# Row sums of an attention softmax: five key blocks on the PE in 384 and 192 columns

## The chip, the cores and the metric

The kernel runs on one core of a Trainium2 chip. The metric is the device time of one execution in microseconds (us), as the median of several runs. The engines are PE (TensorE, matmul), DVE (VectorE), ACT (ScalarE), POOL (GpSimd) and SP (SyncE, which issues every DMA of this kernel, in program order).

## The reference

Three layers follow one another: a causal attention with a forget gate, a dense layer, and a layer of soft experts. Only the attention is touched by the change. It has 4 x 8 = 32 heads of 576 positions and 64 dimensions.

```python
scores = scale * np.matmul(q, k.transpose(0, 1, 3, 2))
log_f = np.log(np.clip(f, 0.0001, 1.0))
cum = np.cumsum(log_f, axis=-1)
decay = cum[:, :, :, None] - cum[:, :, None, :]
scores = np.where(causal, -1000000000.0, scores + decay)
scores = scores - np.max(scores, axis=-1, keepdims=True)
attn = np.exp(scores)
attn = attn / (np.sum(attn, axis=-1, keepdims=True) + 1e-09)
return np.matmul(attn, v)
...
x = attention output, 2304 x 512
h = x @ w_in; g = h * sigmoid(h); y = g @ w_out
soft experts on y: 32 slots, 8 experts, 2304 x 512 out
```

## The kernel before, in words

**Order.** Attention goes head by head: step `i` of `att_step` works on the scores of head `i`, on the row maxima of head `i + 3`, on the splitting of Q and K of head `i + 4`, and on the product with V of the pair of heads `pa` before. A pair takes two steps. The order of the pieces within a step is written out by hand in the string `ORDER` (L18), whose two halves, divided by a bar, are the first and the second step of a pair. Every engine carries out its instructions in that order. In the background the steps also convert a few of the dense layer's weights (`c`).

**Scores.** They are kept transposed: keys on the partitions, queries along the free axis. A head has five key blocks of 128, 128, 128, 128 and 64 keys; because of the causal mask block `kb` holds queries 128 kb to 576 only, so the blocks have 576, 448, 320, 192 and 64 columns. `s_piece` makes two matmuls a piece, ACT takes the exponential from PSUM into SBUF tiles `E[i][kb]` (L244), and POOL zeroes the upper triangle of the diagonal block (L246). `max_piece` (L190 on PE, L196 on DVE) does the row maxima of a later head in three PSUM banks taken in turn (ring "b"), from which `row_sums` takes its bank too.

**Row sums before.** The denominator of the softmax is the sum of `E` over keys, so over partitions and blocks. `e_sum` (L249 to L255, pieces `a0` and `a1` of the step after) adds blocks 0, 1 and 2 on DVE into a tile `ES`. `row_sums` (L262, piece `r` in the first step of a pair) then sums over the partitions with matmuls against a matrix of ones, 32 columns wide, so that four column groups of the PE hold two heads times two halves of 288 queries. Blocks 3 and 4 come from `E` directly. All operands are fp32, and the trace has two MATMUL instructions for each of these matmuls. ACT copies the 128 x 288 result to `RS` (L278), and one DMA spreads one row of each group over a tile `sg` of 128 partitions and 9 columns (L281). The step after, `norm_b` (L308 to L318, piece `n`) takes the reciprocal on DVE, stores it to a DRAM tile `R` with one DMA (L311) and reads it back twice, spread over 64 partitions each (`RB`, L318). `norm_c` (piece `b`) multiplies on DVE (L327).

**Queue behind the gather.** On SP the DMA of `sg` is followed by the load of Q and K of pair `p + 3` (`load`, piece `l0`, L139) into one of two buffers. `split_hi` (pieces `q0`, `q1`; L154 to L158 on ACT) reads that buffer from the beginning of the next pair's first step on.

Of the kernel before, what the change touches and what calls it, by code (L numbers as in the profile page):

```python
# [9 lines left out]
F32 = mybir.dt.float32  # L10
# [3 lines left out]
AF = mybir.ActivationFunctionType  # L14
ALU = mybir.AluOpType
AX = mybir.AxisListType

ORDER = "v0 m0 q0 v1 v2 a0 m1 m2 s0 s1 f0 a1 m3 a2 q1 z0 p s2 a3 s3 m4 r s4 l0 s5 c m5 z1 f1 | q1 q0 v0 v1 s0 l1 f0 f1 s1 a0 s2 z0 b a1 n v2 m0 m1 v3 m2 w s3 m3 s4 a2 z1 m4 s5 m5 a3 c"  # L18
NSUM = 1
# [19 lines left out]
def tile_attention_moe_softmoe(ctx: ExitStack, tc: tile.TileContext, qk, vr, f, wcat, phi, w1, w2, out):  # L39
# [23 lines left out]
    def bank(ring, shape, name):  # L63
        tags = RINGS[ring]
        turn[ring] += 1
        ch = tags[turn[ring] % len(tags)]
        return ps.tile(shape, F32, name=name, tag=("av" if ch in "ab" else "b") + ch, bufs=1)
# [59 lines left out]
    def load(p):  # L127
        b, hp = divmod(p, NP)
        src = qk[b, hp]
        if p == 0:  # L130
            staged[p] = ([UB[:, h] for h in range(2)],
                         [att.tile([128, S], F32, name="ES", tag="ES", bufs=2) for h in range(2)])
            nc.sync.dma_start(out=UB, in_=src[:, 0])
            for h in range(2):
                nc.sync.dma_start(out=staged[p][1][h], in_=src[:, 1, h])
            return
        t = ld.tile([128, 2, 2, S], F32, name="qk", tag="qk", bufs=2)
        staged[p] = [[t[:, c, h] for h in range(2)] for c in range(2)]
        nc.sync.dma_start(out=t, in_=src)  # L139
# [82 lines left out]
    E, ES = {}, {}  # L222
# [26 lines left out]
    def e_sum(i, j):  # L249
        if j == 0:  # L250
            ES[i] = att.tile([128, S], F32, name="ES", tag="ES", bufs=2)
        kb = j + 1
        m = 64 if kb == 4 else 128
        es = ES[i][0:m, 128 * kb:S]
        nc.vector.tensor_tensor(es, E[i][0][0:m, 128:S] if j == 0 else es, E[i][kb][0:m], ALU.add)  # L255

    AVP, U, RT = {}, {}, {}
    SUMS, READY, done = set(), set(), {"r": 0, "n": 0, "b": 0}
    HALF = S // 2
    ES_ = "sum"  # L260

    def row_sums(p):  # L262
        t = bank(RING_T, [128, HALF], "rs")
        parts = [(0, 128, HALF - 128, ES_), (0, 0, 128, 0), (1, HALF, HALF, ES_)]
        parts += [(1, 128 * kb, S - 128 * kb, kb) for kb in range(2 + NSUM, 5)]
        for half, c0, n, src in parts:
            for h in range(2):
                g = 32 * (2 * h + half)
                i = 2 * p + h
                k = 64 if src == 4 else 128  # L270
                rhs = ES[i][:, c0:c0 + n] if src is ES_ else E[i][src][0:k, 0:n]
                c = c0 - half * HALF
                nc.tensor.matmul(t[g:g + 32, c:c + n], lhsT=ones[0:k], rhs=rhs, start=src in (ES_, 0),  # L273
                                 stop=src == 0 or half == 0 or src == (4 if NSUM < 3 else ES_))
        for h in range(2):
            ES.pop(2 * p + h)
        r = att.tile([128, HALF], F32, name="RS", tag="RS", bufs=1)
        nc.scalar.activation(r, t, AF.Copy)  # L278
        sg = nrm.tile([128, 9], F32, name="sg", tag="sg", bufs=2)
        src = bass.AP(tensor=r.tensor, offset=r.offset, ap=[[32 * r.ap[0][0], 4], [1, HALF]])  # L280
        nc.sync.dma_start(out=sg, in_=src)  # L281
        RT[p] = sg
# [23 lines left out]
    def norm_b(p):  # L306
# [4 lines left out]
        nc.sync.dma_start(out=r.rearrange("h (c j) -> (h c) j", j=9), in_=sg)  # L311
# [17 lines left out]
    def att_step(i, cv):  # L329
# [22 lines left out]
        for op in ORDER.split("|")[h].split():  # L352
# [10 lines left out]
            elif k == "a" and 0 <= i - 1 < NH:  # L363
                if int(j) <= NSUM:
                    e_sum(i - 1, int(j))
                if j == "3":
                    SUMS.add(i - 1)
# [689 lines left out]
```

## Time and profile before

| | us |
|---|---|
| median of 3 runs | 629.3 (626.63 to 632.15) |
| profiled execution | 633.63 |
| its span, first to last instruction | 631.9 |
| PE busy | 562.0 (89%) |
| DVE busy | 421.9 (67%) |
| ACT busy | 348.7 (55%) |
| POOL busy | 262.4 (42%) |

The span leaves out what lies around the first and last instruction, so it is a little under the profiled execution's own time. Busy shares are means over the whole span; attention takes about its first 230 us, and the dense layer and the experts the rest. A busy PE is not a PE at its peak, since pipelined matmuls overlap and the end of each is modelled.

### The profile page before, as it was taken

How to read it: one execution, taken by the hardware profiler on the slowest of the kernel's cores; microseconds unless marked ns; L12 is line 12 of the kernel's file. 1: busy time of each engine (PE TensorE's matmuls, PEld its weight loads, DVE VectorE, ACT ScalarE, POOL GpSimd, SP SyncE). 2: the span in 40 equal slices, each digit the busy share in tenths (PEclk: the TensorE clock that was granted, in tenths of full speed). 3: DMA queues.
4: the chain of work that ended last, by engine and by line, in shares of the span. 5: the costliest groups of instructions: out<-in, count | busy, mean ns of one | idle time of the engine just before them, and what ended most of it. 6: DMA issues, size and time to landing. Idle time of an engine off the chain costs nothing.

```text
span 631.9 us, 13040 instructions
## 1 busy us (share of the span) xinstructions
PE 562.0 (89%) x4873; PEld 424.9 (67%) x4873; DVE 421.9 (67%) x1018; ACT 348.7 (55%) x783; POOL 262.4 (42%) x326
## 2 busy tenths in 40 slices
PE   3599999898998976989988999899999999978993
PEld 2476666565565655878876998777888989864542
DVE  7589999999987859999994114668768752322012
ACT  6688898887875656555654334354544633322022
POOL 6369879977967314564442000114334320002000
PEclk9999999999987998798998999999999999999997
DMA  6643564554542138511200022226423126697998
GB/s 207 212 161 129 179 222 133 177 164 155 175 133 65 43 120 297 188 67 67 80 23 0 3 67 67 68 67 233 167 68 129 44 95 198 207 332 263 349 350 273
DMA packets 46098, 94.44 MB, mean 149 GB/s; under 512 B 7858, under 2 KB 29138, under 8 KB 44114
## 3 DMA queue, kind: packets, MB, share of 16 engines
q1 hardware_dynamic: 46034, 93.61, 44.7%
q8 instruction: 38, 0.62, 0.4%
q14 instruction: 26, 0.21, 0.1%
HBM read 87.83 MB, written 4.94 MB: 147 GB/s over the span
## 4 chain that ended last, share of the span: by engine, by line
PE 54%; DVE 22%; ACT 9%; issue 7%; DMA 6%; SPq 0%; POOL 0%; ACTq 0%; DVEq 0%; POOLq 0%
PE h L557 8%; PE h L558 7%; PE h L559 7%; PE av L293 5%; PE mx L190 5%; PE gtp L590 4%; DVE wt L458 3%; DVE g L577 3%; PE st L239 3%; PE lp L604 3%; PE h L779 2%; PE st L241 2%; DVE ES L255 2%; PE rs L273 2%; DVE raw L462 2%
## 5 line engine op out<-in xcount | busy, mean ns | idle before, releaser
L557 PE MATMUL h<-xh,w 128*128 128x256 f32 x576 | 171.8, 298 | 2.0 <-ACT xh L544 2.0
L558 PE MATMUL h<-xl,w 128*128 128x256 f32 x576 | 164.3, 285 | 0.2 <-DVE xl L545 0.2
L559 PE MATMUL h<-xh,w 128*128 128x256 f32 x576 | 164.0, 285 | 0.0
L557 PEld LDWEIGHTS h<-xh,w 128*128 128x128 f32 x576 | 111.3, 193 | 19.4 <-issue 16.0
L577 DVE SCALAR_TENSOR_TENSOR g<-g,h 128x512 f32<-128x512 f32 (+1 forms) x73 | 49.3, 677 | 102.0 <-ACT g L571 102.0
L485 POOL TENSOR_TENSOR raw<-raw 128x512 f32<-128x512 f32 x32 | 40.9, 1279 | 175.5 <-DVE raw L464 99.9
L558 PEld LDWEIGHTS h<-xl,w 128*128 128x128 f32 x576 | 111.5, 194 | 0.4 <-DVE xl L545 0.4
L559 PEld LDWEIGHTS h<-xh,w 128*128 128x128 f32 x576 | 111.3, 193 | 0.0
L593 ACT ACTIVATE gt<-gtp 128x512 f32<-128x512 f32 x72 | 42.4, 589 | 85.9 <-PE gtp L590 85.7
L190 PE MATMUL mx<-KA,QA 127*128 127x256 f32 (+2 forms) x192 | 68.2, 399 | 23.7 <-DMA KA<-cum 9.3
L244 ACT ACTIVATE E<-st 128x256 f32<-128x256 f32 (+2 forms) x192 | 65.0, 382 | 29.1 <-PE st L241 26.9
L196 DVE CUSTOM_DVE_ANT_0 junk<-mx,mask 128x64 bf16<-128x64 f32 (+4 forms) x160 | 63.6, 421 | 21.6 <-PE mx L190 20.7
L246 POOL TENSOR_SCALAR_AFFINE_SELECT E<-E 128x128 f32<-128x128 f32 (+1 forms) x160 | 57.5, 376 | 47.6 <-ACT E L244 41.8
L190 PEld LDWEIGHTS mx<-KA,QA 127*128 127x128 f32 x192 | 38.0, 213 | 48.7 <-issue 17.9
L590 PE MATMUL gtp<-ident,g 128*128 128x128 f32 x288 | 45.5, 282 | 20.7 <-DVE g L577 16.2
L293 PE MATMUL av<-E,VF 128*64 128x320 f32 (+4 forms) x448 | 62.5, 386 | 0.0
L239 PE MATMUL st<-QA,KA 128*128 128x256 f32 (+1 forms) x192 | 61.3, 329 | 0.2
L241 PE MATMUL st<-QB,KB 128*128 128x256 f32 (+1 forms) x192 | 55.8, 305 | 0.0
L458 DVE SCALAR_TENSOR_TENSOR wt<-raw,wt 128x512 int32<-128x512 int32 x48 | 51.8, 1102 | 1.4 <-ACT wt L451 1.4
L451 ACT ACTIVATE wt<-wt,nbias 128x512 int32<-128x512 int32 x48 | 33.5, 720 | 34.6 <-DVE wt L448 34.4
L590 PEld LDWEIGHTS gtp<-ident,g 128*128 128x128 f32 x288 | 33.4, 143 | 23.9 <-DVE g L577 18.8
L168 POOL TENSOR_TENSOR QB<-qk,QB 64x576 fp32r<-64x576 f32 x30 | 43.0, 1434 | 8.2 <-ACT QB L158 5.9
(149 smaller groups left out, 994.5 us busy)
## 6 DMA issues: line engine op xcount, KB each, us to landing
unit<-in_w_dram SPq DMA_DIRECT2D x64, 512.0 KB
raw<-in_w_dram SPq DMA_DIRECT2D x48, 512.0 KB
qk<-in_qk_dram SPq DMA_DIRECT2D x15, 1152.0 KB
VF<-in_v_dram SPq DMA_DIRECT2D x16, 320.0 KB
RB<-R SPq DMA_DIRECT2D x32, 144.0 KB
out_dram<-ob SPq DMA_DIRECT2D x16, 256.0 KB
QA<-QA SPq DMA_DIRECT2D x2, 320.0 KB
UB<-in_qk_dram SPq DMA_DIRECT2D x1, 576.0 KB
```

Source lines behind the costliest of these rows:

```text
L190: nc.tensor.matmul(t[:, 0:n], lhsT=qa[0:127, h, 128 * blk:128 * blk + 128], rhs=ka[0:127, h, k0:k0 + n], start=True, stop=True)
L196: nc.vector.tensor_tensor_reduce(out=junk[:, 0:w], in0=t[:, 0:w], in1=mask[:, 448 - w:448], scale=1.0, scalar=-3e38, op0=ALU.add, op1=ALU.max,
L239: nc.tensor.matmul(t[0:m, 0:n], lhsT=ka[:, h, k0:k0 + m], rhs=qa[:, h, 64 + q0:64 + q1], start=True, stop=False)
L241: nc.tensor.matmul(t[0:m, 0:n], lhsT=kb_[:, h, k0:k0 + m], rhs=qb[:, h, q0:q1], start=False, stop=True)
L244: nc.scalar.activation(e[0:m, c0:c0 + n - skip], t[0:m, skip:n], AF.Exp, scale=0.125)
L293: nc.tensor.matmul(AVP[p][x][64 * h:64 * h + 64, o0:o0 + n], lhsT=VF[p % 2][0:k, kb, h], rhs=E[2 * p + h][kb][0:k, c:c + n], start=kb == 0 ...
L458: v.scalar_tensor_tensor(t, hi, -2147483648, t, op0=ALU.bitwise_and, op1=ALU.bitwise_or)
L557: nc.tensor.matmul(t[:, u], lhsT=a, rhs=xh[:, d], start=(d == 0), stop=False)
L558: nc.tensor.matmul(t[:, u], lhsT=a, rhs=xl[:, d], start=False, stop=False)
L559: nc.tensor.matmul(t[:, u], lhsT=w[:, 1, d * 128:(d + 1) * 128], rhs=xh[:, d], start=False, stop=(d == 3))
L577: nc.vector.scalar_tensor_tensor(g[:, u], g[:, u], 1.0, t[:, u], op0=ALU.add, op1=ALU.mult)
L590: nc.tensor.transpose(tp[:, t, u], g[:, u, t * 128:(t + 1) * 128], ident)
```

## The change

The adds on DVE go: `e_sum`, `ES`, and the pieces `a0`, `a1` (and `a2`, which did nothing) of `ORDER`. `a3` stays and only marks a head as complete. `row_sums` reads all five blocks of both heads from `E`. It cuts the 576 queries at 384: two column groups hold the first 384 queries of the two heads (blocks 0, 1, 2), two hold the last 192 (all five blocks). The copy on ACT, the gather into `sg` (now 96 partitions of 12 columns) and the store to `R` are two instructions each. The tile that holds K of the first pair keeps its size under another name.

```diff
-ORDER = "v0 m0 q0 v1 v2 a0 m1 m2 s0 s1 f0 a1 m3 a2 q1 z0 p s2 a3 s3 m4 r s4 l0 s5 c m5 z1 f1 | q1 q0 v0 v1 s0 l1 f0 f1 s1 a0 s2 z0 b a1 n v2 m0 m1 v3 m2 w s3 m3 s4 a2 z1 m4 s5 m5 a3 c"
-NSUM = 1
+ORDER = "v0 m0 q0 v1 v2 m1 m2 s0 s1 f0 m3 q1 z0 p s2 a3 s3 m4 r s4 l0 s5 c m5 z1 f1 | q1 q0 v0 v1 s0 l1 f0 f1 s1 s2 z0 b n v2 m0 m1 v3 m2 w s3 m3 s4 z1 m4 s5 m5 a3 c"
...
-    def e_sum(i, j):
-        if j == 0:
-            ES[i] = att.tile([128, S], F32, name="ES", tag="ES", bufs=2)
-        kb = j + 1
-        m = 64 if kb == 4 else 128
-        es = ES[i][0:m, 128 * kb:S]
-        nc.vector.tensor_tensor(es, E[i][0][0:m, 128:S] if j == 0 else es, E[i][kb][0:m], ALU.add)
...
-    HALF = S // 2
-    ES_ = "sum"
+    CUT = 384
 
     def row_sums(p):
-        t = bank(RING_T, [128, HALF], "rs")
-        parts = [(0, 128, HALF - 128, ES_), (0, 0, 128, 0), (1, HALF, HALF, ES_)]
-        parts += [(1, 128 * kb, S - 128 * kb, kb) for kb in range(2 + NSUM, 5)]
-        for half, c0, n, src in parts:
-            for h in range(2):
-                g = 32 * (2 * h + half)
...
-        nc.scalar.activation(r, t, AF.Copy)
-        sg = nrm.tile([128, 9], F32, name="sg", tag="sg", bufs=2)
-        src = bass.AP(tensor=r.tensor, offset=r.offset, ap=[[32 * r.ap[0][0], 4], [1, HALF]])
-        nc.sync.dma_start(out=sg, in_=src)
+        t = bank(RING_T, [128, CUT], "rs")
+        for kb in range(5):
+            k = 64 if kb == 4 else 128
+            for half, c0, c1 in ((0, 0, CUT), (1, CUT, S)):
+                q0 = max(c0, 128 * kb)
+                for h in range(2):
+                    g = 32 * (2 * half + h)
+                    if q0 < c1:
+                        nc.tensor.matmul(t[g:g + 32, q0 - c0:c1 - c0], lhsT=ones[0:k],
+                                         rhs=E[2 * p + h][kb][0:k, q0 - 128 * kb:c1 - 128 * kb], start=kb == 0,
+                                         stop=kb == (2, 4)[half])
+        r = att.tile([128, CUT], F32, name="RS", tag="RS", bufs=1)
+        nc.scalar.activation(r[0:64], t[0:64], AF.Copy)
+        nc.scalar.activation(r[64:128, 0:S - CUT], t[64:128, 0:S - CUT], AF.Copy)
+        sg = nrm.tile([96, 12], F32, name="sg", tag="sg", bufs=2)
+        for half, p0, n in ((0, 0, CUT), (1, 64, S - CUT)):
+            row = r[64 * half:64 * half + 1]
+            src = bass.AP(tensor=row.tensor, offset=row.offset, ap=[[32 * r.ap[0][0], 2], [1, n]])
+            nc.sync.dma_start(out=sg[p0:p0 + n // 6], in_=src)
...
-        nc.sync.dma_start(out=r.rearrange("h (c j) -> (h c) j", j=9), in_=sg)
+        for c0, c1, p0 in ((0, CUT, 0), (CUT, S, 64)):
+            nc.sync.dma_start(out=r[:, c0:c1].rearrange("h (c j) -> h c j", j=12), in_=sg[p0:p0 + (c1 - c0) // 6])
...
             elif k == "a" and 0 <= i - 1 < NH:
-                if int(j) <= NSUM:
-                    e_sum(i - 1, int(j))
-                if j == "3":
-                    SUMS.add(i - 1)
+                SUMS.add(i - 1)
```

## Rows read from the trace of the kernel before

**Rows 1.** The page: shares of the chain that ended last, by engine.

```profile
PE 54%; DVE 22%; ACT 9%; issue 7%; DMA 6%; SPq 0%; POOL 0%; ACTq 0%; DVEq 0%; POOLq 0%
```

**Rows 2.** Windows: length, busy PE, PEld, DVE, ACT, POOL; granted clock; DMA.

```profile
48.57:121.56 72.99, 69.33 (x512) 44.66 (x510) 70.54 (x207) 63.73 (x154) 64.41 (x91) 1.00 0.53 173
121.56:160.89 39.33, 35.96 (x259) 22.29 (x255) 37.38 (x108) 31.67 (x76) 30.73 (x45) 1.00 0.48 154
160.89:227.76 66.87, 61.05 (x429) 40.41 (x429) 53.99 (x152) 45.88 (x117) 41.52 (x69) 0.90 0.31 97
...
167.00:179.00 12.00, 10.96 (x56) 7.31 (x59) 10.36 (x30) 7.54 (x19) 8.44 (x13) 0.72 0.46 154
194.00:207.00 13.00, 10.76 (x56) 7.20 (x60) 9.95 (x29) 5.59 (x16) 7.17 (x12) 0.74 0.16 49
178.90:190.08 11.18, 11.18 (x87) 7.31 (x86) 10.47 (x32) 10.29 (x25) 8.96 (x14) 1.00 0.43 137
```

**Rows 3.** Timeline of ACT: start us, us; the first AV half's copy, one a pair.

```profile
48.57 0.36 ACT L298 ACTIVATE UB<-av 128x256 f32<-128x256 f32 x1
...
121.56 0.38 ACT L298 ACTIVATE UB<-av 128x256 f32<-128x256 f32 x1 [0.15 <-PE av L293]
```

**Rows 4.** The adds in the groups by line; then the chain in three stages.

```profile
L255 DVE TENSOR_TENSOR ES<-E 128x448 f32<-128x448 f32 x32 | 32.6, 1019 | 1.5 <-POOL E L246 1.5
L255 DVE TENSOR_TENSOR ES<-ES,E 128x320 f32<-128x320 f32 x32 | 21.4, 669 | 0.5 <-POOL E L246 0.2
...
by line: PE mx L190 13.7%; issue 12.3%; PE av L293 10.9%; DVE ES L255 8.8%; DVE junk L196 7.0%; DVE raw L462 6.0%; DVE x L327 5.6%; PE st L239 5.0%; PE st L241 4.9%; ACT E L244 4.2%; PE rs L273 3.7%; DVE wt L458 2.6%; DVE Mx L193 2.0%; ACT 
by line: DMA qk<-in_qk_dram 16.7%; issue 14.5%; DVE wt L458 9.1%; PE av L293 8.8%; PE rs L273 6.9%; DVE ES L255 6.6%; PE mx L190 6.3%; DVE junk L196 5.6%; PE st L239 5.3%; DVE x L327 4.9%; PE st L241 3.3%; ACT E L244 2.3%; DVE raw L460 2.2%
by line: PE av L293 23.2%; PE mx L190 14.6%; PE st L239 12.5%; PE st L241 9.5%; PE rs L273 9.1%; DVE x L327 5.8%; issue 4.8%; DVE ES L255 4.3%; DVE sg L308 2.3%; DVE junk L196 2.2%; PE h L558 1.8%; PE h L559 1.4%; DVE Mt L209 1.3%; PE h L55
```

**Rows 5.** Waits between 38 and 160.89: us in total, times, longest.

```profile
PEld rs L273 <- DVE ES L255: 3.8, 7, 1.2
ACT QA L157 <- DMA qk<-in_qk_dram: 3.1, 4, 1.4
ACT RS L278 <- issue: 3.0, 2, 1.6
```

**Rows 6.** Timeline of PE around one call of row_sums; chain in the expert layer.

```profile
178.91 0.70 PE L273 MATMUL rs<-ES,ones 128*32 128x160 f32 x7
...
180.10 0.39 PE L239 MATMUL st<-QA,KA 128*128 128x256 f32 x1
...
579.31 8.84 PE h L779 x160
```

**Rows 7.** Timeline of ACT over one pair: start us, us.

```profile
96.88 0.68 ACT L157 ACTIVATE QA<-qk 64x576 fp32r<-64x576 f32 x1 [1.39 <-DMA qk<-in_qk_dram]
...
101.15 0.41 ACT L278 ACTIVATE RS<-rs 128x288 f32<-128x288 f32 x1
...
108.44 0.67 ACT L157 ACTIVATE QA<-qk 64x576 fp32r<-64x576 f32 x1
```

**Rows 8.** Groups by line: copies of ACT from PSUM; busy us, mean ns.

```profile
L300 ACT ACTIVATE UB<-av 128x320 f32<-128x320 f32 x16 | 6.6, 415 | 3.3 <-PE av L293 3.3
...
L298 ACT ACTIVATE UB<-av 128x256 f32<-128x256 f32 x16 | 5.9, 370 | 6.2 <-PE av L293 6.2
```

**Rows 9.** Timeline of SP's queue in that pair: start us, us of issue.

```profile
101.59 0.62 SPq L281 DMA_DIRECT2D sg<-RS  x1
102.30 0.43 SPq L139 DMA_DIRECT2D qk<-in_qk_dram  x1
...
106.67 0.34 SPq L311 DMA_DIRECT2D R<-sg  x1
```

**Rows 10.** The chain before the second fall of the clock: start us, us.

```profile
195.01 1.81 DVE x L327 x2
196.82 0.75 DVE ES L255
```

More of the change, by code (lines that the diff above doesn't have):

```diff
@@ L131, in load @@
             staged[p] = ([UB[:, h] for h in range(2)],
-                         [att.tile([128, S], F32, name="ES", tag="ES", bufs=2) for h in range(2)])
+                         [att.tile([128, S], F32, name="k0", tag="k0", bufs=2) for h in range(2)])
             nc.sync.dma_start(out=UB, in_=src[:, 0])
@@ L220, in max_fin_b @@
                           in_=mr[0:5 * n].bitcast(F32))
-    E, ES = {}, {}
+    E = {}
     SP = [(0, 0, 256, 0), (0, 256, 576, 0), (1, 128, 576, 0), (2, 256, 576, 0), (3, 320, 576, 64), (4, 512, 576, 0)]
@@ L260, in tile_attention_moe_softmoe @@
-    ES_ = "sum"
+    CUT = 384
     def row_sums(p):
-        t = bank(RING_T, [128, HALF], "rs")
-        parts = [(0, 128, HALF - 128, ES_), (0, 0, 128, 0), (1, HALF, HALF, ES_)]
-        parts += [(1, 128 * kb, S - 128 * kb, kb) for kb in range(2 + NSUM, 5)]
-        for half, c0, n, src in parts:
-            for h in range(2):
-                g = 32 * (2 * h + half)
[L269 to L277, printed above, removed]
-        nc.scalar.activation(r, t, AF.Copy)
-        sg = nrm.tile([128, 9], F32, name="sg", tag="sg", bufs=2)
-        src = bass.AP(tensor=r.tensor, offset=r.offset, ap=[[32 * r.ap[0][0], 4], [1, HALF]])
-        nc.sync.dma_start(out=sg, in_=src)
+        t = bank(RING_T, [128, CUT], "rs")
[17 more added lines that the diff above has]
+            nc.sync.dma_start(out=sg[p0:p0 + n // 6], in_=src)
```

## The prediction

> **What bounds the kernel now.** I read the page's chain of waits first [rows 1]: PE has 54% of the path, DVE 22%, ACT 9%. The change touches attention only, so I then cut the span there by stage [rows 2], at the starts of the copy of the first AV half (L298), one per pair of heads; the first and the last of the seven of stage 1 stand in [rows 3], and the bounds of the later stages are the next such copies. Six pairs take 72.99 us, 12.17 each, with DVE busy 70.54 of it (11.76 a pair, 97%) and PE 69.33. Three more take 39.33 (13.11 each, DVE 95%); the last five, with less work per pair, 66.87. In stage 1 DVE has no slack; PE is close behind, but its busy time includes the tail of pipelined matmuls, so I looked for a pair in which PE never waits: from 178.90 to 190.08 it is busy for 11.18 of 11.18 us [rows 2]. That is PE's floor for a pair as it is now, 1.0 us under what stage 1 takes.
>
> The chain by stage [rows 4] says what the removed work holds: the adds (DVE ES L255) are 8.8% of stage 1 (6.4 us), 6.6% of stage 2 (2.6 us) and 4.3% of stage 3 (2.9 us): 11.9 us of the path, the most that can come back from them directly. Row sums on PE (rs L273) are 3.7%, 6.9% and 9.1%, or 2.7, 2.7 and 6.1 us.
>
> **Removed: the adds.** 32.6 + 21.4 = 54.0 us of DVE over 16 pairs [rows 4], 3.38 a pair. DVE falls from 11.76 to 8.4 us a pair in stage 1 and stops being the bound. The rs matmuls no longer wait for DVE: 3.8 us over 7 waits between 38 and 160.89 [rows 5]. The DVE steps behind the adds in program order (multiply x, reciprocal sg, the next max pieces) start up to 3.4 us earlier in a pair, and with them the PE pieces that wait for a bank of theirs.
>
> **Added on PE.** One call of row_sums starts at 178.91 and the next full-width matmul follows at 180.10: 1.19 us [rows 6]. Each fp32 matmul is two passes. The busier pair of its four column groups carries 288 + 192 + 64 columns, 1088 over two passes; the other pair 576. What a column costs with four groups side by side is read from the expert layer, 160 passes of 256 columns in 8.84 us [rows 6]: 55 ns each, so 221 ns for four at once and 0.863 ns a column in a group. 1088 columns make 0.94 us, and 0.25 us are start, the change to 64 rows and the drain. After the change the groups carry 384 + 256 + 128 = 768 and 4 x 192 + 64 = 832 columns; the busier one needs 1664 x 0.863 = 1.44, with the same 0.25 it is 1.69 us: **+0.50 us a pair**. Bounds: below, +0.50 less the wait for DVE that goes (3.8 over 7 is 0.54), so nothing; above, if the groups do not overlap more than one block with the next, 3200 x 0.863 + 0.25 = 3.01 us, +1.82. I take +0.50, since the old call itself fits the rate of the expert layer.
>
> **Added on ACT.** One copy of 288 columns, 0.41 us [rows 7], becomes one of 384 and one of 192. Copies of 320 and 256 columns take 415 and 370 ns [rows 8], 0.70 ns a column: 460 + 325 = 785, **+0.37 us a pair**. ACT is 63.73 of 72.99 busy in stage 1. At least nothing (other work of PE goes on), at most 14 x 0.37 = 5.2 us. In the three stages I count it on the path in three pairs: +1.2. Behind these copies on ACT stand the exponentials of the step's last pieces and the splits of Q and K.
>
> **Added on SP.** The gather of the sums (sg) is one issue of 0.62 us and becomes two; the store R 0.34, also two [rows 9]. Right behind sg on SP is the load of the Q and K of a later pair (L139). Its bytes come back at the head of the next pair, where ACT waits for them (L157): 3.1 us in 4 waits [rows 5]. The cost is between nothing (the first gather can be issued while ACT copies the second half) and 0.62 a pair; I take nothing for the forecast, because in that window of ten pairs it waited 4 times only, and keep the other end as a rival. The second R costs 0.34 in front of the last weight loads after attention: +0.4, at least nothing. The new shape of sg (96 x 12 for 128 x 9) changes two small DVE operations; the time that the removed adds leave on DVE covers that, and without it the next max pieces would wait for them as they do now.
>
> **The sum.** Stage 1: PE's floor becomes 11.18 + 0.50 = 11.68; 6 x (12.17 - 11.68) = -2.9. Stage 2: two copies of the sums came so late there that ACT stood 3.0 us [rows 5], behind adds that ended late. Floor plus 0.3 for a load that is still late, 12.0 a pair: -3.3. Stage 3: the adds on the path go (-2.9), five row sums get longer (+2.5), and the clock counts. The granted clock there is 0.72 over 167 to 179 and 0.74 over 194 to 207 [rows 2]: TensorE at the lower of its levels (1.2 for 2.4 GHz) for part of each, after PE had been idle (it is busy 10.96 of 12 and 10.76 of 13). (1 - 0.72) x 12 and (1 - 0.74) x 13 are 3.4 us each of full-speed time. Ahead of the second fall the path lies on DVE, with multiply and add one after the other [rows 10]; I count one of the two falls as saved, -3.4. Stage 3: -3.8. With +1.2 (ACT) and +0.4 (R): **-8.4 us**. Everything behind attention shifts with it. The profiled execution took 633.63 (span 631.9 and 1.73 around it), 4.3 above the median 629.3; its sum gives 625.2, and against the median 620.9. I predict **621 us**.
>
> **Rivals.** *PE is the bound already, and DVE's relief turns into DVE idle time.* For: PE busy 69.33 of 72.99, and the longer row sums lie where PE never waits. Against: the floor of 11.18 has room for 0.50. Stage 1 and 2 then give only half, -3.1, stage 3 -0.4 (adds against row sums, no clock), +1.6 elsewhere: about -2, **627 us**.
>
> *The chain of the next load becomes the bound (slower).* In one pair ACT's split starts at 96.88, the sums are copied at 101.15 [rows 7], the load is issued at 102.30 [rows 9], and the next split starts, without a wait, at 108.44: 11.56 us round. With +0.50 (PE), +0.37 (ACT) and up to +0.62 (second gather) it is 12.4 to 13.1, more than the 12.17 of a pair. At +0.9 for each of the 12 pairs with a load behind the gather it is +11: **640 us**. It decides once the bytes land after ACT reaches the split, which they did 4 times. Against: the rs wait that goes takes about 0.5 out of the same round, and the load may have landed well before 108.44. The Trainium skill ("DMA: Bandwidth & Descriptors", Rules for kernel authors) advises against two transfers to separate partition halves, because they serialize: by that the whole second issue counts, and the round would stand at the upper end. No row shows two gathers in a row.
>
> *DVE's relief comes in full and the clock stays up.* -11.9 for the adds, -6.8 for both falls of the clock, +4 for row sums and copies on the path: -15, **614 us**. For: the idle time of PE ahead of the second fall is DVE's [rows 10].
>
> *The four groups do not run side by side.* If each second pass held up all that is behind it, a call would take the 3.01 us above, and the floor 13.0 a pair: +5 in stage 1, nothing in stage 2, +9 in stage 3, +4 in the first pairs, **647 us**. The Trainium skill ("TensorE: Matmul & The Clock Gate", Step-by-step: what each phase is for) has it that matmuls stay in program order and only weight loads are pulled ahead. The 55 ns per pass of 256 columns [rows 6] speak against it: that order would give twice as much.
>
> **How the numbers follow.** Forecast 0.45, PE bound 0.28, load chain 0.13, full relief 0.10, no overlap 0.04. The range takes in the first, second and fourth case, with ACT's upper bound (+4 on 627) as its upper end: **613 to 632**; the slower two, 0.17, are left out. A measurement of this kernel can tell about 1% from no change, so 623.0 and 635.6 are the marks. The forecast, within some 4 us of its sum, lies below 623 with about 0.8 (0.36), the full relief always: faster 0.46. Same: the rest of the forecast and the PE rival, 0.37, and a little of the load chain, 0.39 in all. Slower: 0.15.
>
> **What would show it.** Right: DVE near 8.4 us a pair in stage 1 and PE nearly without idle time; rs calls of about 1.7 us that start without a wait; pairs of 11.7; no lower clock before 228 us or one fall fewer; the attention part 8 us shorter and the rest as before. Wrong: rs calls near 3 us; ACT's split waiting for the load in most pairs; pairs still at 12.1 with DVE idle; a clock that falls somewhere else, in attention or in the stage of converting weights behind it, and takes back what attention gained.

## The result and the profile after

| | before | after |
|---|---|---|
| median of 20 runs, us | 630.67 (626.63 to 636.82) | 624.61 (620.78 to 628.47) |
| ratio, 95% interval | | 0.9896 [0.9873, 0.992] |
| profiled execution, us | 633.63 | 622.81 |
| PE / DVE / ACT busy, us | 562.0 / 421.9 / 348.7 | 555.2 / 379.3 / 355.0 |

The kernel became 6.1 us faster by the medians, whose quotient is 0.9904; the ratio in the table is an estimate of its own. The prediction was 621 in a range of 613 to 632, from a sum of -8.4. The two profiled executions differ by 10.8, more than the medians, so the trace has to be read by stage before any of it is believed.

The page after: busy time and share of each engine, then the chain that ended last by engine.

```profile
PE 555.2 (89%) x5065; PEld 424.3 (68%) x5065; DVE 379.3 (61%) x954; ACT 355.0 (57%) x799; POOL 256.8 (41%) x326
...
PE 56%; DVE 16%; ACT 13%; DMA 6%; issue 5%; POOL 1%; SPq 1%; ACTq 0%; DVEq 0%; POOLq 0%
```

Against [rows 1] DVE lost 6 points of the path, PE took 2 of them and ACT 4. That ACT took twice what PE did is a first sign of where the forecast erred.

Windows of after, columns as in [rows 2]: the start, the three stages (cut at the same copy of the first AV half, now L288), the 112.24 us behind attention (weight conversion), the last 292 us (they overlap the stretch before by 3.3), and the two stretches of time in which the clock had fallen before the change.

```profile
0.00:50.82 50.82, 32.45 (x167) 22.66 (x167) 29.56 (x100) 35.50 (x71) 27.45 (x43) 1.00 0.55 180
50.82:125.71 74.89, 70.47 (x592) 47.24 (x591) 57.49 (x190) 66.33 (x160) 60.51 (x91) 1.00 0.51 169
125.71:161.11 35.40, 34.08 (x288) 22.30 (x287) 27.52 (x88) 32.60 (x79) 28.90 (x45) 1.00 0.52 171
161.11:220.19 59.08, 55.78 (x486) 37.98 (x486) 40.20 (x130) 47.37 (x123) 40.38 (x69) 1.00 0.34 110
220.19:332.43 112.24, 95.03 (x855) 81.89 (x852) 97.52 (x162) 66.17 (x126) 54.88 (x37) 0.94 0.33 116
329.10:621.00 291.90, 270.71 (x2720) 215.29 (x2719) 127.64 (x287) 108.20 (x248) 44.65 (x45) 0.99 0.49 161
167.00:179.00 12.00, 11.21 (x98) 7.38 (x96) 9.75 (x34) 10.63 (x27) 10.40 (x18) 1.00 0.45 153
194.00:207.00 13.00, 13.00 (x115) 8.65 (x113) 9.03 (x30) 8.07 (x25) 7.55 (x16) 1.00 0.18 52
```

The same cuts of before, where [rows 2] doesn't have them:

```profile
0.00:48.57 48.57, 30.61 (x155) 21.72 (x155) 33.86 (x105) 34.80 (x70) 28.03 (x42) 1.00 0.57 189
227.76:340.00 112.24, 93.97 (x808) 80.19 (x805) 98.52 (x161) 64.37 (x122) 53.06 (x37) 0.91 0.33 116
340.00:632.00 292.00, 271.11 (x2723) 215.60 (x2721) 127.66 (x287) 108.26 (x248) 44.67 (x45) 0.99 0.49 161
```

Attention, up to the last of these copies, takes 220.19 for 227.76: -7.6. The last 292 us are alike. The other 3.3 us (10.9 in the spans less 7.6) lie in the conversion of weights, which has the same work in both, at a granted clock of 0.94 for 0.91: a difference between two single executions, and the medians, 6.1 apart, don't bear it out.

Inside attention the signs differ: the start +2.3, stage 1 **+1.9** (forecast -2.9), stage 2 -3.9 (forecast -3.3), stage 3 -7.8 (forecast -3.8). DVE's relief is there everywhere: in stage 1 it is busy 57.49 of 74.89, 9.6 us a pair for 11.76. But the pair got longer, 12.48 for 12.17. How far a single trace can be trusted here is seen from two kernels below whose time differs from the old and the new one's by nothing measurable: with the load in two halves the old kernel's start and stages take 48.38, 73.35, 39.14 and 64.45, the new one's 48.20, 74.73, 34.88 and 61.58. Stages 1 and 2 repeat within 0.6 us; the start and stage 3 move by up to 2.6, so the +2.3 of the start may be chance.

The new operations. First the chain of waits of after around one call of row_sums (start us, us), then ACT's copies in the groups by line and shape, then SP's queue in one pair (start us, us of issue):

```profile
102.28 1.69 PE rs L261 x24
103.97 0.31 PE st L238
```

```profile
L265 ACT ACTIVATE RS<-rs 64x384 f32<-64x384 f32 x16 | 7.7, 483 | 7.0 <-PE rs L261 3.3 <-ACT E L243 2.3 <-issue 1.3
L266 ACT ACTIVATE RS<-rs 64x192 f32<-64x192 f32 x16 | 5.2, 326 | 0.4
```

```profile
104.60 1.24 SPq L271 DMA_DIRECT2D sg<-RS  x2
105.89 0.41 SPq L138 DMA_DIRECT2D qk<-in_qk_dram  x1
...
109.41 1.26 SPq L302 DMA_DIRECT2D R<-sg  x2
```

The call takes 1.69 us, as forecast, and so does each of the other 15. The two copies take 809 ns (forecast 785), the two gathers 1.24 us of issue for 0.62, the two stores 1.26 for 0.34 [rows 9].

The waits of after between 38 and 160.89, us in total, times, longest:

```profile
PE mx L189 <- ACT mr L217: 6.2, 10, 1.1
...
DVE sg L298 <- DMA sg<-RS: 5.0, 5, 1.6
...
ACT QA L156 <- DMA qk<-in_qk_dram: 4.6, 8, 2.1
```

and PE's before:

```profile
PE mx L190 <- DVE Mt L196: 3.7, 7, 0.8
PE mx L190 <- ACT mr L218: 1.8, 7, 0.3
```

The waits of rs for the adds [rows 5] are gone, and they were larger than they look. The windows of stage 1 with the row sums alone (length, busy PE, PEld, ACT), before and then after:

```profile
48.57:121.56 72.99, 9.96 (x120) 4.76 (x120) 2.47 (x6) 1.00 0.53 173
50.82:125.71 74.89, 10.55 (x192) 6.12 (x192) 4.86 (x12) 1.00 0.51 169
```

Six calls hold PE nearly as long before as after. The call of 1.19 us in [rows 6] is one of four among the 16 that didn't wait inside; the others took 1.32 to 2.49. In the pair of [rows 7] the first matmul of the call starts at 99.35, the first head's; the weight load for the second head's waits for that head's add until 99.77, and the profile counts PE as busy meanwhile. From the first matmul of a call to the next other matmul the 16 calls take 25.6 us before and 27.0 after.

In place of the waits for DVE, PE waits once in every pair for `mr`: the row maxima are transposed on PE into one of the three banks of ring "b", ACT copies them out, and the next piece of row maxima needs that bank. Between 38 and 160.89 PE waits there 6.2 us for 1.8. This is how one such wait comes about, in ACT's timeline of after (start us, us; idle time before an instruction stands in brackets):

```profile
91.80 0.48 ACT L265 ACTIVATE RS<-rs 64x384 f32<-64x384 f32 x1 [0.47 <-ACT E L243]
92.31 0.33 ACT L266 ACTIVATE RS<-rs 64x192 f32<-64x192 f32 x1
92.66 0.43 ACT L243 ACTIVATE E<-st 128x192 f32<-128x192 f32 x2
...
96.28 0.36 ACT L243 ACTIVATE E<-st 128x256 f32<-128x256 f32 x1
96.55 0.25 ACT L217 ACTIVATE mr<-mtp 10x128 fp32r<-10x128 f32 x1
```

and in PE's:

```profile
96.85 0.42 PE L189 MATMUL mx<-KA,QA 127*128 127x320 f32 x1 [1.08 <-ACT mr L217]
```

From the copies of the sums to `mr` ACT has no idle time: what the copies take longer, `mr` comes later, and PE stands 1.08 us until it is there.

### The profile page after: what moved, and what is told of

Same layout as the page of the kernel before. It is cut to its first block, busy times and chain, and to the rows that moved or that the text cites. A ratio compares the mean times of both kernels' runs of the same rounds, so it can differ in the third digit from the quotient of the medians.

```text
span 621.0 us, 13351 instructions
## 1 busy us (share of the span) xinstructions
PE 555.2 (89%) x5065; PEld 424.3 (68%) x5065; DVE 379.3 (61%) x954; ACT 355.0 (57%) x799; POOL 256.8 (41%) x326
## 4 chain that ended last, share of the span: by engine, by line
PE 56%; DVE 16%; ACT 13%; DMA 6%; issue 5%; POOL 1%; SPq 1%; ACTq 0%; DVEq 0%; POOLq 0%
PE h L545 8%; PE h L546 7%; PE h L547 7%; PE av L283 5%; PE mx L189 5%; PE st L238 4%; PE rs L261 3%; PE gtp L578 3%; DVE g L565 3%; PE st L240 3%; DVE wt L446 3%; PE lp L592 2%; PE h L767 2%; DVE wt L436 2%; ACT E L243 2%
## 5 line engine op out<-in xcount | busy, mean ns | idle before, releaser
L195 DVE CUSTOM_DVE_ANT_0 junk<-mx,mask 128x64 bf16<-128x64 f32 (+4 forms) x160 | 65.7, 426 | 44.0 <-PE mx L189 41.7
L189 PE MATMUL mx<-KA,QA 127*128 127x256 f32 (+2 forms) x192 | 65.3, 384 | 22.0 <-DMA KA<-cum 9.3
L245 POOL TENSOR_SCALAR_AFFINE_SELECT E<-E 128x128 f32<-128x128 f32 (+1 forms) x160 | 53.8, 353 | 47.5 <-ACT E L243 45.6
L243 ACT ACTIVATE E<-st 128x256 f32<-128x256 f32 (+2 forms) x192 | 63.5, 379 | 16.0 <-PE st L240 14.6
L283 PE MATMUL av<-E,VF 128*64 128x320 f32 (+4 forms) x448 | 60.5, 376 | 0.0
L446 DVE SCALAR_TENSOR_TENSOR wt<-raw,wt 128x512 int32<-128x512 int32 x48 | 44.4, 949 | 1.4 <-ACT wt L439 1.4
```

Source lines behind the costliest of these rows:

```text
L189: nc.tensor.matmul(t[:, 0:n], lhsT=qa[0:127, h, 128 * blk:128 * blk + 128], rhs=ka[0:127, h, k0:k0 + n], start=True, stop=True)
L195: nc.vector.tensor_tensor_reduce(out=junk[:, 0:w], in0=t[:, 0:w], in1=mask[:, 448 - w:448], scale=1.0, scalar=-3e38, op0=ALU.add, op1=ALU.max,
L243: nc.scalar.activation(e[0:m, c0:c0 + n - skip], t[0:m, skip:n], AF.Exp, scale=0.125)
L283: nc.tensor.matmul(AVP[p][x][64 * h:64 * h + 64, o0:o0 + n], lhsT=VF[p % 2][0:k, kb, h], rhs=E[2 * p + h][kb][0:k, c:c + n], start=kb == 0 ...
L446: v.scalar_tensor_tensor(t, hi, -2147483648, t, op0=ALU.bitwise_and, op1=ALU.bitwise_or)
```

## The experiments

Ratios are to the kernel before, in the same session, with a 95% interval; 0.0016 is 1 us. In the theories, the change is taken as three parts: DVE's adds go, PE's row sums get longer, ACT and SP get a second copy, gather and store. Stage times are those of single profiled executions, cut as above.

**Load of Q and K issued earlier, in the new kernel.** If the round copy, gather, load, split sets the pair, an earlier load breaks it.

```diff
-"... q1 z0 p s2 a3 s3 m4 r s4 l0 s5 c m5 z1 f1 | ..."
+"... q1 z0 p l0 s2 a3 s3 m4 r s4 s5 c m5 z1 f1 | ..."
```

> The changed kernel with one step moved: the load of Q and K of pair p + 3 (l0) stands right behind the small load p of the same step, ahead of row_sums, so it no longer waits on SP behind the two gathers. Theory A (in the changed kernel the round split, row sums, copy, gathers, load, next split is what sets the length of a pair): ACT's split no longer waits for the load (12 waits of some 0.4 to 2 us now, to at most 2), a pair of the nine of stages 1 and 2 falls from 12.25 to about 11.7 us (PE's floor with the longer row sums), and the time by about 6 us, to 618 to 619 (ratio to the kernel before about 0.980). Rival B (PE or ACT sets the length, and the load comes in just in time because they are slow): the load lands early, the waits go, and the time stays at 624 to 625 (0.990).

Measured: 643.66, ratio 1.0163 [1.0125, 1.0202]: slower, which no theory had. The chain of waits of this kernel, and its waits between 38 and 160.89:

```profile
94.81 6.52 DMA sg<-RS
...
123.76 5.08 DMA sg<-RS
```

```profile
DVE sg L298 <- DMA sg<-RS: 19.8, 9, 5.8
...
PEld mx L189 <- DVE Mt L195: 11.6, 9, 2.9
```

The gather of the sums, 4.5 KB, is now issued behind the load of 1152 KB and lands 5 to 6.5 us later. DVE waits for it with everything behind it in its queue, and PE waits for DVE's maxima. The move put a new wait in, so the run says nothing on the round it was meant to break.

**The same move in the kernel before.** The control: same edit of the order, in the old string.

> The kernel before with the same move of the load alone. Theory A: there the bound of a pair was DVE (97% busy), and the load waited for in 4 of 10 pairs by 3.1 us; moving it gains at most those, 0 to 3 us, 627.5 to 630.5 (ratio 0.995 to 1.0). Rival B (the round of the load bound the kernel before as much as it binds the changed one): it gains 6 us as well, to 624 to 625 (0.990), and what the change gains beyond the move is then the same as without it.

Measured: 633.74, 1.0035 [0.9999, 1.0071]. Here DVE waits for `sg` 1.0 us in 2 waits instead of 19.8 in 9: with the adds ahead of it in its queue it comes to the reciprocal late anyway. The transfer is late there too (4.17 and 4.57 us in its chain of waits), so it seems that a busier DVE hid it.

**The adds put back, unused, into the new kernel.** This parts DVE's relief from everything else the change brings.

```diff
+    def e_sum(i, j):
...
+        nc.vector.tensor_tensor(es, E[i][0][0:m, 128:S] if j == 0 else es, E[i][kb][0:m], ALU.add)
...
-                SUMS.add(i - 1)
+                if int(j) <= 1:
+                    e_sum(i - 1, int(j))
+                if j == "3":
+                    SUMS.add(i - 1)
```

> The changed kernel with the old adds on DVE put back in their old places; nobody reads their result. It pays all the costs of the change (row sums +0.50, copies +0.4, second gather +0.65 us a pair) and has no relief of DVE; only the wait of the row sums for the adds is gone. Theory A: a pair is bound by the longer round of the load with DVE's delays in it, so slower than the kernel before by 3 to 8 us, 634 to 639 (1.005 to 1.013), with falls of the clock in the last pairs again. Rival C (the relief of DVE gives nothing; the gain is that the row sums no longer wait for the adds, or the better split of the columns): equal to the changed kernel, 624 to 626 (0.990).

Measured: 632.41, 0.9993 [0.9961, 1.0026], between the two expectations. With the adds in, nothing of the gain is left: it takes DVE's relief to have any. That the rest comes out even doesn't show that each part of it is free. The row sums no longer wait inside a call for the adds, which makes up for most of their longer matmuls (PE is busy with them for 10.55 us in stage 1, as in after, for 9.96 before). PE's wait for `mr` in stage 1 is there with the adds in place, 4.2 us for 1.3 before:

```profile
PE mx L189 <- ACT mr L217: 4.2, 6, 1.1
```

In this trace stage 1 takes 76.24 for 72.99 and stage 2 37.68 for 39.33. So the added copy makes PE wait in stage 1 also while DVE is as busy as before (69.71 us for 70.54); where in the kernel that is made good, one trace doesn't show.

**The adds gone from the old kernel, nothing added.** The opposite half. Block 0 of `E` is read in place of `ES`, so the sums lack blocks 1 and 2; the matmuls are as many and as large as before.

```diff
-                rhs = ES[i][:, c0:c0 + n] if src is ES_ else E[i][src][0:k, 0:n]
+                rhs = E[i][0][:, c0:c0 + n] if src is ES_ else E[i][src][0:k, 0:n]
...
-                if int(j) <= NSUM:
-                    e_sum(i - 1, int(j))
-                if j == "3":
-                    SUMS.add(i - 1)
+                SUMS.add(i - 1)
```

> The kernel before with the adds left out and nothing put in their place: row_sums has the matmuls of before, with block 0 in place of the added tile, so blocks 1 and 2 are left out of the row sums. It has the relief of DVE with no cost on PE, ACT and SP. Theory A: the adds gave 11.9 us of the path, of which the round of the load (11.2 to 11.9 us without stalls) and PE's floor of 11.2 a pair let some 8 to 12 come back, with no fall of the clock in the last pairs: 617 to 622 (0.979 to 0.986); the difference to the changed kernel, 3 to 8 us, is what the new row sums cost. Rival D (DVE was not the bound): 628 to 631.

Measured: 614.49, 0.9723 [0.9699, 0.9747]: -17.5 us, more than expected. Start and stages:

```profile
0.00:47.49 47.49, 29.17 (x155) 20.14 (x155) 29.39 (x100) 34.66 (x71) 27.36 (x42) 1.00 0.59 193
47.49:116.06 68.57, 66.32 (x512) 43.80 (x510) 54.99 (x183) 62.43 (x153) 58.10 (x89) 1.00 0.55 184
116.06:151.38 35.32, 33.85 (x262) 22.30 (x259) 27.51 (x95) 30.96 (x77) 30.73 (x47) 1.00 0.50 172
151.38:209.19 57.81, 55.19 (x426) 37.42 (x426) 39.27 (x130) 44.44 (x118) 39.12 (x69) 0.97 0.35 112
```

A pair of stage 1 takes 11.43, near the floor of 11.18 that the prediction read from one pair. Every call of row_sums takes 1.19 us here, 19.0 in all for 25.6 before. The difference, 6.6, is what PE waited inside these calls, as much as a third of the relief. So the change gives up over half of what it frees: 17.5 freed and, by the ratio 0.9896, 6.6 kept. The next two runs put the two other parts on this kernel one at a time.

**Plus the new matmuls alone.** As the run before, with the row sums of after; one copy of 192 columns, one gather and one store, so that a part of the sums isn't passed on. The copy takes 0.33 us for 0.42, so PE's part may come out a little small.

```diff
-        t = bank(RING_T, [128, HALF], "rs")
+        t = bank(RING_T, [128, CUT], "rs")
+        for kb in range(5):
...
-        r = att.tile([128, HALF], F32, name="RS", tag="RS", bufs=1)
-        nc.scalar.activation(r, t, AF.Copy)
+        r = RSK
+        nc.scalar.activation(r[:, 0:192], t[:, 0:192], AF.Copy)
```

> No adds, and of the new work that of PE alone: the matmuls of the changed row_sums (five blocks, 384 and 192 columns), but one copy (of 192 columns, the first groups' other 192 are left out of the sums), one gather and one store as before. To be held against the kernel with the adds gone and nothing added, 614.5 us. Theory A2 (with the adds gone a pair is as long as the round split, row sums, copy, gathers, load, next split): the row sums lie in that round, +0.5 less 0.08 for the shorter copy, in 12 pairs, and +0.5 in the last three: +6 us, 620 to 621 (ratio to the kernel before 0.982). Rival B2 (PE's continuous work is the bound instead): +0.5 in each of 15 pairs, +7 to +8, 622 (0.986). This one alone does not part the two; the next does.

Measured: 619.63, 0.9831 [0.979, 0.9872]. Against the run with the adds gone that is +0.0108, about 7 us (the two intervals together leave some 3 to either side): PE's part costs what was expected.

```profile
49.25:121.22 71.97, 70.71 (x595) 47.46 (x591) 56.89 (x192) 63.74 (x153) 60.09 (x91) 1.00 0.53 176
```

In stage 1 the pair goes from 11.43 to 12.00, +0.57, with PE busy 98% of it.

**Plus copy, gather and store in two, alone.** As the run with the adds gone, old matmuls.

```diff
-        nc.scalar.activation(r, t, AF.Copy)
+        for h in range(2):
+            nc.scalar.activation(r[64 * h:64 * h + 64], t[64 * h:64 * h + 64], AF.Copy)
...
-        nc.sync.dma_start(out=sg, in_=src)
+        for h in range(2):
+            row = r[64 * h:64 * h + 1]
+            src = bass.AP(tensor=row.tensor, offset=row.offset, ap=[[32 * r.ap[0][0], 2], [1, HALF]])
+            nc.sync.dma_start(out=sg[64 * h:64 * h + 64], in_=src)
```

> No adds, the matmuls of the kernel before (block 0 in place of the added tile, so blocks 1 and 2 are left out of the sums), but copy, gather and store split in two by heads: the cost of the change on ACT and SP with nothing added on PE. Held against 614.5 us. Theory A2: from the copy to the issue of the load 1.15 becomes 1.75 us, in 12 pairs: +7 us, 621 to 622 (0.984), with ACT's split waiting for the load in every pair. Rival B2 (PE is the bound): the load comes later but nobody waits: 614 to 616 (0.973 to 0.976).

Measured: 618.89, 0.9808 [0.9774, 0.9843]: +0.0085, 5.4 us (some 2.7 to either side), where the prediction had counted 1.6; the time lies between the two expectations. Stage 1 of this kernel in the windows, then PE's wait for `mr` between 38 and 160.89 in this kernel, then the same wait in the one with the new matmuls alone:

```profile
48.85:119.97 71.12, 66.09 (x512) 43.85 (x510) 54.00 (x184) 65.79 (x159) 58.19 (x89) 1.00 0.55 178
```

```profile
PE mx L190 <- ACT mr L218: 7.4, 10, 1.1
```

```profile
PE mx L192 <- ACT mr L220: 1.8, 7, 0.3
```

PE does the same work as with the adds gone (66.09 busy for 66.32), but the pair takes 0.43 longer: about what the second copy adds on ACT here (two copies of 402 ns for one of 417). The wait for `mr` comes with this part of the change, not with the matmuls.

**The order opened up.** The load at the head of the pair (with the small load `p`) and the reciprocal (`n`) a step later, to give every transfer of the round a whole pair.

```diff
-"v0 m0 q0 v1 v2 m1 m2 s0 s1 f0 m3 q1 z0 p s2 a3 s3 m4 r s4 l0 s5 ... z0 b n v2 ..."
+"v0 m0 q0 p l0 v1 v2 m1 m2 s0 s1 n f0 m3 q1 z0 s2 a3 s3 m4 r s4 s5 ... z0 b v2 ..."
```

> The changed kernel with the round opened at both ends: the loads p and l0 move to the head of the pair's first step, ahead of the gathers on SP, and the reciprocal n of the pair before moves from the second step to the next pair's first, so that a gather that lands behind the load holds up nobody. In the run with the load moved alone the gather landed 5 to 6.5 us after its issue, and DVE and then PE stood for it. Theory A2: no waits for the load nor for the gather, pairs of 11.7 us (PE's floor) for 12.25: about 6 us less than the changed kernel, 618 (0.980). Rival B2 (PE or ACT is the bound already): 624 to 625 (0.990). Were the time above 630, the moved steps have a cost of their own.

Measured: 661.22, 1.0481 [1.0443, 1.0519]. A miss of the same kind as the first run: the store `R` is now the one behind the load. Its chain of waits, and the wait at the end of it (38 to 160.89):

```profile
113.90 4.50 DMA R<-sg
...
119.02 2.97 DMA RB<-R
122.08 0.91 DVE x L318 x3
```

```profile
DVE x L318 <- DMA RB<-R: 28.7, 7, 6.0
```

**The same in the kernel before.**

> The kernel before, adds kept, with the same three moves as in the run above. Theory A2: a pair was bound by DVE there and the waits for the load were 3.1 us: 0 to 4 us less, 627 to 631 (0.994 to 1.0). If it gains as much as the changed kernel does, the round bound both alike.

Measured: 662.49, 1.049 [1.0453, 1.0527]. Here the kernel before loses as much: the late `RB` holds up the multiply in both (20.4 us in 6 waits here). These two runs show what this order costs, a load ahead of a small transfer and a later reciprocal together, and nothing on the change.

**The load in two halves, Q first, in the new kernel.** This lifts the wait of ACT's split without moving anything.

```diff
-        nc.sync.dma_start(out=t, in_=src)
+        for c in range(2):
+            nc.sync.dma_start(out=t[:, c], in_=src[:, c])
```

> The changed kernel with the load of Q and K cut into two DMAs at the same place on SP, Q first, so nothing is issued in another order and nothing urgent stands behind more bytes than before. ACT's next split needs Q only, K half a step later. Theory A2 (the round split, row sums, copy, gathers, load, next split sets the length of a pair): Q lands about 2 us earlier, the round falls from 12.2 to some 10 us and PE's floor with the longer row sums, 11.7, takes over: 5 to 6 us less than the changed kernel, 618 to 620 (ratio to the kernel before 0.981). Rival B2 (PE or ACT is the bound): 624 to 625 (0.990). In the two runs in which the load moved ahead of small transfers, those landed up to 5 us late; here they do not.

Measured: 624.01, 0.9888 [0.9847, 0.9929], no different from the change itself. The waits between 38 and 160.89:

```profile
PE mx L190 <- ACT mr L218: 5.9, 10, 0.8
...
ACT QA L157 <- DMA qk<-in_qk_dram: 2.4, 2, 1.2
```

The split waits 2.4 us in 2 waits for 4.6 in 8, and the time stays. The load round is nearly tight in after, but it doesn't set the pair. The wait for `mr` is nearly untouched.

**The same in the kernel before.**

> The kernel before, adds kept, with the load cut in the same two halves. Theory A2: DVE sets the length of a pair and the waits for the load were 3.1 us in ten pairs, so 0 to 3 us less, 627 to 631 (0.995 to 1.0). If it gains as much as the changed kernel, the round bound both alike, and the change's own gain is not cut by it.

Measured: 631.56, 1.0017 [0.9993, 1.0042]: nothing, as expected of a control.

**The two copies of the sums on DVE instead of ACT, in the new kernel.** If ACT's queue is the cost, this should give it back, since DVE has time.

```diff
-        nc.scalar.activation(r[0:64], t[0:64], AF.Copy)
-        nc.scalar.activation(r[64:128, 0:S - CUT], t[64:128, 0:S - CUT], AF.Copy)
+        nc.vector.tensor_copy(r[0:64], t[0:64])
+        nc.vector.tensor_copy(r[64:128, 0:S - CUT], t[64:128, 0:S - CUT])
```

> The changed kernel with its two copies of the row sums from PSUM made by DVE, which has room now, and no longer by ACT. Theory F (what the second copy costs is ACT's queue: between 38 and 160 us PE stood 6.2 us for the small copy mr, which is queued on ACT behind copies and splits, against 1.8 in the kernel before; the run with copies and gathers split shows 7.4, the run with PE's cost alone 1.8): PE's waits for ACT fall to 2 us or less and the time by 4 to 8 us against the changed kernel, 617 to 621 (ratio to the kernel before 0.977 to 0.984). Theory G (the round of the load stands just behind, at 12.2 us a pair): the waits for ACT go but the waits for the load grow in their place, 622 to 625 (0.987 to 0.991). Theory H (PE's own work bounds a pair): no gain either, and neither wait.

Measured: 630.21, 0.996 [0.9923, 0.9996]: slower than the change, and outside what any of the three theories gave. The waits between 38 and 160.89:

```profile
DVE RS L265 <- PE rs L261: 12.7, 10, 1.3
...
PE mtp L215 <- DVE Mt L208: 9.3, 10, 1.2
...
PEld mx L189 <- ACT mr L217: 0.7, 3, 0.2
```

The wait for `mr` is all but gone, as it should be if ACT's queue makes it. But DVE, with its slack, reaches the copy before PE has finished the sums, stands 12.7 us in 10 waits, and the maxima behind it in its queue come late to PE: 9.3 us in 10 waits. One wait was exchanged for a larger one. Stage 1 stays as long as in after, 74.80; stages 2 and 3 take 38.09 and 63.35 for 35.40 and 59.08.

**Both, copies on DVE and the load in halves.**

> The same, and the load of Q and K cut into two DMAs, Q first: ACT's queue and the round of the load are both relieved. Alone the cut load gave nothing (0.9888 against 0.9896). Theory F: as the run before, 617 to 621. Theory G (two bounds of nearly the same height, of which either holds when the other is lifted): only this run gains, to 615 to 619 (0.975 to 0.982), with pairs of 11.7 us in stages 1 and 2, PE's floor with the longer row sums. Theory H: 622 to 625 with pairs of 12 us, PE busy throughout and no wait of note.

Measured: 632.12, 0.9998 [0.9966, 1.0029]. The two waits of the run before are there unchanged (12.7 and 9.3), so the load had nothing to give. No version here that passes on the whole sums beats the changed kernel.

## Why the prediction was right, and where it erred

The sign and the range held: -6.1 us with an interval of -8.0 to -5.0 (0.0127 and 0.008 of 630.67), forecast -8.4. By the prediction's own mark of 1% the result is on the line between faster, to which it gave 0.46, and the same, 0.39. The terms can now be checked one by one, since the three parts were run apart. In the table a part is the difference of two profiled executions, us; the forecast of the relief is its terms without the longer row sums (stage 1: 6 x (11.18 - 12.17) = -5.9).

| | start | stage 1 | stage 2 | stage 3 | sum | forecast |
|---|---|---|---|---|---|---|
| adds gone | -1.1 | -4.4 | -4.0 | -9.1 | -18.6 | -5.9 - 4.8 - 6.3 = -17.0 |
| new matmuls | +1.8 | +3.4 | -1.5 | +2.4 | +6.1 | +3.0 + 1.5 + 2.5 = +7.0 |
| copies, gathers, stores | +1.4 | +2.6 | +1.2 | +0.1 | +5.2 | +1.2 |
| the three together | +2.0 | +1.5 | -4.3 | -6.6 | -7.3 | -8.8 |
| after less before | +2.3 | +1.9 | -3.9 | -7.8 | -7.6 | -8.8 |

The parts add up to the whole within 0.3 us in the traces, and within the intervals in the ratios too: 0.9723 + 0.0108 + 0.0085 = 0.9916, beside 0.9896 [0.9873, 0.992]. So no further effect is needed to account for the change. An agreement as close as 0.3 is luck, since the start and stage 3 of a single trace move by some 2.5 us. A part of the +3.4 in stage 1 and the -1.5 in stage 2 is work that changed sides: three max pieces more lie on stage 1's side of the cut in after, and four in the kernel with the new matmuls alone.

**The relief of DVE: right.** -17.5 by the ratio, -18.6 in the traces, -17.0 in the terms. Its spread was off: 1.5 less in stage 1, where the floor of 11.18 wasn't quite reached (11.43), and 2.8 more in stage 3, where the clock rose from 0.90 to 0.97 over the whole stage. In after both falls are gone, and not one. The granted clock is 1.00 in the two windows that had 0.72 and 0.74 [rows 2], and in the second PE is busy 13.00 of 13.00, for 10.76. The clock of stage 3 as a whole is 0.90 before, 0.92 to 0.97 in the kernels whose adds stay (early load in the kernel before 0.97, load in halves there 0.95, adds kept in the new one 0.92), 0.97 to 1.00 in the table's kernels without them. With the load in halves and the copies on DVE, without the adds, it is 0.95, and 0.94 with the order opened up. One profile stands for each and the two groups touch, so it goes with the adds, but that they are its cause isn't shown.

**PE's part: right.** The call was forecast at 1.69 us and takes 1.69, and +7.0 stands beside +6.1 and +6.8. That a column costs 0.863 ns in each of four groups at once, read from the expert layer [rows 6], carried over to groups of unequal length. Beside the calls of the old kernel, most of which waited inside for the adds, they grew by 1.4 us in all and not by 8; the prediction has that wait in its lower bound for the row sums, and its sum has it in the relief. By the rule of the Trainium skill that matmuls stay in program order ("TensorE: Matmul & The Clock Gate", Step-by-step: what each phase is for), if that meant one after another across column groups too, the call would have taken 3.01; the trace disagrees with that reading.

**ACT's and SP's part: mis-sized, and this is the term that failed.** "In the three stages I count it on the path in three pairs: +1.2" and 0.4 for the stores. Its price per pair was right (+0.40 for ACT, +0.62 for the gather); the number of pairs was wrong. The prediction names no row for its three pairs (three times 0.37 is 1.1), and the old profile has PE waiting for `mr` only 1.3 us in all of stage 1. But PE waits on ACT's queue in every pair, through the bank that `mr` empties, and the longer copies push `mr` back each time: +0.43 a pair in stage 1. The price is 5.4 us instead of 1.6. The waits of PE in stage 1, us, say where it is paid (idle is the length less busy PE; the wait for `mr` is from the waits of the same window):

| kernel | a pair | PE idle | of it for `mr` |
|---|---|---|---|
| before | 12.17 | 3.66 | 1.3 |
| adds gone | 11.43 | 2.25 | 1.8 |
| with the new matmuls | 12.00 | 1.26 | 1.3 |
| with copies, gathers, stores | 11.85 | 5.03 | 4.9 |
| after | 12.48 | 4.42 | 4.2 |
| after, load in halves | 12.46 | 4.43 | 4.0 |
| after, copies on DVE | 12.47 | 5.68 | 0.2 |

The two lines that the reading rests on most are from the windows of stage 1, with copies, gathers and stores first, then after:

```profile
PE mx L190 <- ACT mr L218: 4.9, 6, 1.1
```

```profile
PE mx L189 <- ACT mr L217: 4.2, 6, 1.1
```

The wait for `mr` grows by 3 us wherever ACT makes the two copies, and with the adds kept it is 4.2 as well, so it isn't DVE's relief that brings it. It goes when DVE makes them, with the gathers still in two, and stays when the load lands earlier; so in stage 1 it comes from the copies, and not from the second gather. With the new matmuls alone stage 1 takes 71.97, and after is 2.9 longer, as much as the wait grew. Stage 1 came out 4.8 above its forecast (70.1): 2.6 of that is this term, and 1.5 the relief that fell short. How the rest of the 5.4 us, outside stage 1, divides between the copies and the transfers isn't settled: gathers alone were not run, and the copies moved to DVE brought a wait of their own. The waits of DVE for `sg`, 5.0 us in after, are no sign for the gather, since DVE has slack there. The Trainium skill ("DMA: Bandwidth & Descriptors", Rules for kernel authors) has it that two transfers to separate halves of the partitions serialize. Their issues on SP do follow one another here, 1.24 us for two and 0.62 for one; no run here shows whether the transfers themselves do, or what it costs the kernel.

**The rivals.** *PE already the bound*: false. With the adds gone and PE's work unchanged the kernel is 17.5 us faster; its number, 627, was near for another reason. *The load chain as the bound*: its form came true, the split waits in 8 pairs for 4 before, but not its effect; lifting the wait gives nothing. Nor does the second gather bring these waits: with the adds gone and one gather they are as many (8, 5.7 us). *Full relief at 614*: the relief is that (614.49 with the adds gone), but "+4 for row sums and copies on the path" was too little; they cost 11 by the ratio of after to it, 12 by the two parts apart. *Groups not side by side*: false, 1.69 us.

Of the signs that the prediction named, the call of 1.7 us without a wait and the missing falls of the clock came true; DVE at 8.4 us a pair (9.6; in stage 1 the adds had taken 854 and 717 ns, 3.1 a pair and not the mean of 3.38, and the window of after holds three more max pieces) and pairs of 11.7 with PE never idle (12.48, 0.74 idle) did not. Two of its signs of being wrong came true: ACT's split waits for the load in most pairs, and pairs are above 12.1 with DVE idle (57.49 busy of 74.89). That the sum came so near is in part luck: stage 3 gave 4.0 more than expected and stage 1 4.8 less.

What stays open is how much of the 5.4 us could be had back. A pair of stage 1 is PE's work, 11.75, and 0.74 idle, of which 0.7 is the wait for `mr`; but neither way tried of relieving ACT shortened it without a new wait, so what lifting that wait alone would give isn't shown.

## What to carry to other kernels

Price work that is taken off the bound engine at its full relief, waits inside other engines' instructions included: with the adds gone 17.5 us came back, and as much as a third of it was PE waiting inside its own row sums. Then follow everything that is added to whoever waits behind it, in every pair, and not only in a few, however small its waits in the old profile: 1.6 us counted for three pairs and the stores were 5.4. A balance of nothing (0.9993 with the adds kept) can hide a cost and a saving. Try the two halves of such a change apart, adds gone and costs added, because the difference says how much of the freed time is still to be had. Work with slack beside it isn't free either: an operation moved to an engine that runs ahead of the producer makes that engine's queue wait.

## What the runs showed of the hardware

A small transfer issued on SP's queue behind a load of 1152 KB lands late. The gather of `sg` took 6.52 and 5.08 us behind the load in the new kernel, 4.17 and 4.57 in the old; not behind it, 1.66 with the load in halves and 1.66 to 2.23 with the adds kept. With the order opened up the store `R` took 4.50 to 4.72 us in the chain of waits behind the load, and 1.79 in a late pair that has no load in front:

```profile
113.90 4.50 DMA R<-sg
...
232.61 1.79 DMA R<-sg
```

What that costs depends on who waits: the load moved ahead of the gather cost 2.7% of the new kernel (1.0163 beside 0.9896) and nothing clear of the old (1.0035). The order opened up, in which the reciprocal moved too, cost 5 to 6% of either (1.0481 for 0.9896, 1.049 for 1). In these runs the place of a transfer on its queue was part of its latency.
